# Converting w_out first, a second bank and an early split for its product with w3, two banks from the fourth token block on, and a planner that weighs the shared port

## The chip, the cores and the metric

The kernel runs on one core of one Trainium2 chip. The metric is device time in microseconds (us). In what follows PE is the matrix engine and PEld its weight load, DVE the vector engine, ACT the scalar engine, POOL GpSimd, SP the queue that issues the DMAs.

## The reference

Three layers follow one another: causal block attention (4 batches, 8 heads, 576 tokens, head size 64), then a gated product without activation, then a layer with an ELU.

```python
x = attention(q, k, v)            # block mask of 64, softmax; 2304 tokens x 512
a = x @ w1;  b = x @ w2           # 512 -> 1024
h = a * b @ w3                    # 1024 -> 1024
x = h @ w_out                     # 1024 -> 512
h = x @ w_in                      # 512 -> 2048
g = where(h > 0, h, exp(min(h, 0)) - 1)
out = g @ w_out2                  # 2048 -> 512
```

## The kernel before, in words

**Numbers in two parts.** Every matrix that PE multiplies in the second and third layer is held as a high part that PE reads exactly and a low part (the rest); a product is three matmuls (`PASSES`). Splitting activations costs a cast (ACT) and a subtraction (POOL). The weights come as 64-bit words; `convert` (L293) makes a unit of 128x512 of them: a DMA into a ring of four landing buffers, two ACT instructions (L322, L315), three DVE instructions (L328, L331, L336), one on POOL (L342 or L345), and for two-part results a cast on ACT (L373) and a subtraction on POOL or DVE (L351).

**Stage 1.** Sixteen attention units (`attention`, batch b and head pair hp), each with scores (L483, L538), maxima on DVE (L501, L546), exponentials on ACT (L508, L558), transposes on PE (L518, L569, L579), the product with v (L599), and reciprocals that go through a small transpose (L628) and DRAM before POOL scales the result (L650). Meanwhile 40 units of weights are converted: w_out (8), w3 (16), w1 and w2 together (16, `w12_units`). w_out and w3 are only multiplied with each other: `w_product` (L658) forms one of eight strips of w3 x w_out with 8 matmuls of 128x512 (two instructions each on PE) into the PSUM tile `wps` in bank 6, and splits it with an ACT cast (L677) and a DVE subtraction (L680). w3 strips lie in a ring of four (`RW`), and the slabs of w3 and w_out are taken over by the last weights of w1 and w2. So the second layer needs two products with weights per token, a, b (L767) and y (L731).

**Stage 2.** `block2(t)` handles 288 tokens, t = 0 to 7: split the input (`xs`, L707 on DVE, L712 on POOL; one buffer), eight times a, b and their product, and y in three parts (`PARTS`) of four outputs each; y is collected in `xy` by ACT (L745) or DVE (L751). Blocks 0 to 3 (`few`) use one PSUM bank each for a, b and y (5, 6, 7); from block 4 on each has two (5 and 0, 6 and 1, 7 and 3), of which 0, 1 and 3 belong to attention before. In the meantime the 32 units of the third layer's weights are converted; 12 of 16 slabs go to DRAM and come back when block 7 releases their place.

**Stage 3.** `block3(t)`, 384 tokens, six blocks: h (L839), ELU, split, and out (L874). Its inputs are split by L813 and L818 (`xa`, `xb`).

**What sets the order.** `Plan.run` (L125) lays all operations out once, at build time: each has an engine (some have a choice, `ways`), a cost, a priority (`prio`, smaller first) and dependences. Whenever an engine is free it gets the ready operation of smallest priority, and the engines then execute their lists in that order. Operations with `port=True` on DVE and POOL exclude each other in this calculation. Attention units 1 to 4 have priority -2500 and up, products -2400 and up, all conversions of stage 1 -1000 and up, later attention units 40 and up, PE's work of stage 2 10000 and up, and what empties PSUM in stage 2 about -10000. While PE would have nothing to do, and until the first product, the plan puts in filler matmuls (`spare`, L975).

```python
t = max(free[e], min(o.ready for o in ready[e]))
o = min((o for o in ready[e] if o.ready <= t), key=lambda o: (o.prio, o.n))
if o.ways[e][2]:
    t = max(t, port["POOL" if e == "DVE" else "DVE"])
```

Of the kernel before, what the change touches and what calls it, by code (L numbers as in the profile page):

```python
# [81 lines left out]
class Plan:  # L82
# [6 lines left out]
    def add(self, eng, us, fn, r=(), w=(), prio=0.0, port=False, after=(), lag=0.0, nbytes=0, ways=()):  # L89

        o = Op()
        o.eng, o.us, o.fn, o.prio, o.lag, o.nbytes = eng, us, fn, prio, lag, nbytes
        o.ways = {e: x for e, *x in ((eng, us, fn, port), *ways)}
        o.n = len(self.ops)
        deps = set(after)
        for key in r:
            if key in self.writer:
                deps.add(self.writer[key])
        for key in w:
            if key in self.writer:  # L100
                deps.add(self.writer[key])
            deps.update(self.readers.get(key, ()))
        for key in {*r, *w}:
            buf = key[0] if isinstance(key, tuple) else key
            if isinstance(buf, Buf):
                if key in w and buf.prev is not None:
                    deps.update(buf.prev.ops)
                elif buf.gate is not None:
                    deps.add(self.writer[buf.gate])
                buf.ops.append(o)  # L110
        for key in r:
            if key not in w:
                self.readers.setdefault(key, set()).add(o)
        for key in w:
            self.writer[key], self.readers[key] = o, set()
        deps.discard(o)
        o.deps, o.users = deps, []
        self.ops.append(o)
        return o
# [5 lines left out]
    def run(self):  # L125
        for o in self.ops:
            o.left, o.ready = len(o.deps), 0.0
            for d in o.deps:
                d.users.append(o)
        engines = ("GATE", "PE", "DVE", "ACT", "POOL", "SP")  # L130
        free = dict.fromkeys(engines, 0.0)
        ready = {e: [] for e in engines}
        for o in self.ops:
            if not o.left:
                for e in o.ways:
                    ready[e].append(o)
        pipe, port, done, lanes = 0.0, {"DVE": 0.0, "POOL": 0.0}, 0, [0.0] * self.LANES
        while done < len(self.ops):
            best = None
            for e in engines:  # L140
                if not ready[e]:
                    continue
                t = max(free[e], min(o.ready for o in ready[e]))
                o = min((o for o in ready[e] if o.ready <= t), key=lambda o: (o.prio, o.n))
                if o.ways[e][2]:
                    t = max(t, port["POOL" if e == "DVE" else "DVE"])
                if best is None or t < best[0]:
                    best = t, e, o
            t, e, o = best
            if e == "PE" and self.filler:  # L150
                self.filler(int((t - free[e] - 0.3) / 0.22))
            o.us, o.fn, shared = o.ways[e]
            o.eng = e
            for x in o.ways:
                ready[x].remove(o)
            if e == "SP":
                t = max(t, lanes.pop(0))
                pipe = max(pipe, t + 1.9) + o.nbytes / 390e3
                o.end, free[e] = pipe + 0.3, t + 0.45
                lanes.append(o.end)  # L160
            else:
                o.end = free[e] = t + o.us
                if shared:
                    port[e] = o.end
            o.fn()
            done += 1
            for u in o.users:
                u.ready = max(u.ready, o.end + (0.0 if [*u.ways] == [e] != ["SP"] else self.LAT[e] + u.lag))
                u.left -= 1
                if not u.left:  # L170
                    for x in u.ways:
                        ready[x].append(u)
        self.end = free
# [3 lines left out]
def attention_moe_moe2(  # L177
# [11 lines left out]
    nc = tc.nc  # L189
# [11 lines left out]
    add = plan.add  # L201
# [33 lines left out]
    def bank(k, base):  # L235
        banks[k] = Buf(lambda: psum, f"bank{k}", base, [P, 512], F32, banks[k])
        return banks[k]
# [3 lines left out]
    def turn(name, ks, base):  # L241
        n = turns.get(name, 0)
        turns[name] = n + 1
        return bank(ks[n % len(ks)], base)
# [15 lines left out]
    def wsl(s):  # L260
        return slab_buf[s]()
# [3 lines left out]
    W_S, WO_S, W3_S, RW = 0, 4, 6, 4  # L265
    w12_s = [8, 9, 10, 11, 6, 7, 4, 5]

    def full(s, i):
        return half_buf[s + i // 2]()[:, i % 2]

    def full_keys(s, i):
        return [(half_buf[s + i // 2], i % 2, h) for h in range(2)]
# [8 lines left out]
    def key3(m, x, h):  # L281
        return (hi_buf[m], x, h) if m < 4 else (slab_buf[order3[m - 4]], x, h)
# [373 lines left out]


    def w_product(i, prio):  # L658
        ps = turn("w", (6,), "wps")
        for j in range(KF):  # L660

            def mm(j=j):
                plan.filler = None
                a = full(W3_S, i % RW).rearrange("p (j c) -> p j c", c=P)
                bb = full(WO_S, j // 2).rearrange("p (j c) -> p j c", c=DM)[:, j % 2, :]
                nc.tensor.matmul(ps(), lhsT=a[:, j, :], rhs=bb, start=(j == 0), stop=(j == KF - 1))  # L666

            add(
                "PE", 0.86, mm,
                r=[*full_keys(W3_S, i % RW), *full_keys(WO_S, j // 2)], w=[ps], prio=prio,  # L670
            )

        def d():
            return wsl(W_S + i // 2).rearrange("p s (j c) -> p s j c", c=DM)[:, :, i % 2, :]

        k = [(slab_buf[W_S + i // 2], x, i % 2) for x in range(2)]
        add("ACT", 0.58, lambda: nc.scalar.copy(d()[:, 0, :], ps()), r=[ps], w=[k[0]], prio=prio)  # L677
        add(
            "DVE", 0.68,
            lambda: nc.vector.tensor_tensor(out=d()[:, 1, :], in0=ps(), in1=d()[:, 0, :].bitcast(F32), op=ALU.subtract),  # L680
            r=[ps, k[0]], w=[k[1]], prio=prio,
        )


# [12 lines left out]
    def block2(t):  # L697
# [6 lines left out]
        for k in range(KD):  # L704
# [3 lines left out]
                r=[(x, k, "n")], w=[(xs, k, 0)], prio=fast, port=True,  # L708
# [6 lines left out]
                r=[(x, k, "n"), (xs, k, 0)], w=[(xs, k, 1), (x, k, "s", h2)], prio=fast, port=True,  # L715
            )
        gs = []
        few = t < 4
        abanks, bbanks, ybanks = ((5,), (6,), (7,)) if few else ((5, 0), (6, 1), (7, 3))
        nm_ = "" if few else "+"  # L720

# [33 lines left out]
        for m in range(KF):  # L755
# [4 lines left out]
            def proj(ps, u, pr, m=m, wk=wk):  # L760
# [24 lines left out]
                r=[pb], w=[af], prio=fast,  # L785
# [128 lines left out]
    cp = -1000.0  # L914
    for n in range(NPAIR):
        attention(n, None)
    for h in range(2):
        for s in range(4):
            c = slice(h * 256, (h + 1) * 256)
            convert(  # L920
                wo_r[s][:, :, c], lambda x, s=s, c=c: full(WO_S, s).rearrange("p (j c) -> p j c", c=DM)[:, :, c],
                [[full_keys(WO_S, s)[h]]], cp, True,
            )

    def w12_units(ms, prio):
# [4 lines left out]
    for i in range(KF):  # L930
        for h in range(2):
            c = slice(h * HS, (h + 1) * HS)
            convert(
                w3T[i][:, c], lambda x, i=i, c=c: full(W3_S, i % RW)[:, c], [[full_keys(W3_S, i % RW)[h]]], cp + i, True
            )
        w_product(i, -2400.0 + i)
# [5 lines left out]
    for t in range(N2):  # L942
        block2(t)
    plan.gate("gate2", plan.ops[n1 - 1:])
    first3 = [block3_in(t) for t in range(2)]
    for m in range(KG):
        for h in range(2):
            if m < 4:
# [7 lines left out]
                r=[(st, 0), (st, 1)], w=[("wsc", m, h)], prio=2000.0 + m, nbytes=P * HS * 8,  # L956
            )
        if m >= 4:
            add(
                "SP", 0, lambda m=m: nc.sync.dma_start(out=slab3(m).bitcast(F32), in_=wsc[m - 4]),  # L960
                r=[("wsc", m, h) for h in range(2)], w=[key3(m, x, h) for x in range(2) for h in range(2)],
                prio=5000.0 + m, nbytes=P * 1024 * 8,
# [70 lines left out]
```

## Time and profile before

| | |
|---|---|
| median of 3 runs | 1012.65 us (1009.61 to 1014.29) |
| the profiled execution, its own time | 1009.9 us |
| its span, first to last instruction | 1008.1 us |
| mean granted clock of PE | 0.993 of 2.4 GHz |
| PE busy | 973.1 us (97% of the span) |
| DVE busy | 514.9 us (51%) |
| ACT busy | 425.2 us (42%) |
| POOL busy | 401.0 us (40%) |

A share over the whole span mixes stages of very different load; the rows below go by stretches. A busy PE is not the same as a useful one: the fillers count as busy, and matmuls are pipelined, so what a group of matmuls really takes is read from the distance between the starts of long groups.

### The profile page before, as it was taken

The page shows a single profiled execution, that of the slowest core. Times are in us where ns is not written, and L with a number is a line of the kernel's source. Part 1 is how long each engine was busy: PE and PEld are TensorE (multiplying, and loading weights), DVE is VectorE, ACT ScalarE, POOL GpSimd, SP SyncE. Part 2 cuts the span into 40 slices and gives each one's busy share as a digit, 9 for nine tenths or more (in the row PEclk, how much of TensorE's full clock was granted, in tenths as well). Part 3 has the DMA queues.
Part 4 walks back from the last instruction along what each step waited for, and adds up shares of the span by engine and source line. Part 5 has one row for each costly group of instructions (what it writes and reads, how often), then busy time and mean ns, then how long its engine had stood idle before and what let it go on. Part 6 is the DMA issues. An engine that isn't in the chain of part 4 may idle for free.

```text
span 1008.1 us, 16417 instructions
## 1 busy us (share of the span) xinstructions
PE 973.1 (97%) x6271; PEld 837.7 (83%) x6271; DVE 514.9 (51%) x998; ACT 425.2 (42%) x1017; POOL 401.0 (40%) x403
## 2 busy tenths in 40 slices
PE   9989799999999998999999999999999999999997
PEld 4544348888888898899999988888889988999996
DVE  6888798666565646677566142232332322422222
ACT  6676576655565534544544212222222222222222
POOL 4444565333233136767677232232232422322222
PEclk9999999999999999999999999999999999999999
DMA  6554652221221112355644860000000000000000
GB/s 222 172 162 160 195 169 88 72 73 48 72 71 49 37 55 84 126 172 175 210 157 166 300 243 1 1 32 1 1 32 1 22 11 1 32 1 1 33 1 31
DMA packets 39678, 87.64 MB, mean 87 GB/s; under 512 B 3744, under 2 KB 13360, under 8 KB 38064
## 3 DMA queue, kind: packets, MB, share of 16 engines
q1 hardware_dynamic: 39600, 86.60, 25.9%
q8 instruction: 49, 0.80, 0.3%
q14 instruction: 29, 0.24, 0.1%
HBM read 69.21 MB, written 17.38 MB: 86 GB/s over the span
## 4 chain that ended last, share of the span: by engine, by line
PE 83%; DVE 9%; DMA 4%; issue 1%; ACT 1%; POOL 1%; SPq 0%; POOLq 0%; ACTq 0%; DVEq 0%
PE o L874 20%; PE h L839 20%; PE b L767 10%; PE a L767 10%; PE y L731 9%; PE o L599 4%; PE s L483 3%; PE t L518 3%; DMA cr<-w 2%; DVE ct L336 1%; PE spare L975 1%; DMA scr<-rs 1%; DVE ct L328 1%; PE wps L666 1%; PE s L538 1%
## 5 line engine op out<-in xcount | busy, mean ns | idle before, releaser
L693 POOL TENSOR_TENSOR g<-e,g 128x384 fp32r<-128x384 f32 x96 | 97.6, 1017 | 277.8 <-ACT g L690 266.0
L851 DVE TENSOR_SCALAR e<-h 128x384 f32<-128x384 f32 x96 | 53.5, 557 | 225.3 <-PE h L839 224.8
L874 PE MATMUL o<-slab_lo,g 128*128 128x512 f32 x648 | 160.5, 396 | 0.8 <-POOL g L693 0.4
L855 ACT ACTIVATE e<-e 128x384 f32<-128x384 f32 x96 | 50.4, 525 | 241.8 <-DVE e L851 241.8
L874 PEld LDWEIGHTS o<-slab_lo,g 128*128 128x128 f32 x648 | 121.2, 188 | 26.7 <-POOL g L693 0.8
L731 PE MATMUL y<-g,slab_lo 128*128 128x288 f32 x768 | 120.4, 301 | 6.6 <-DVE xy L751 6.5
L767 PE MATMUL a<-xs,slab_lo 128*128 128x288 f32 x768 | 118.2, 298 | 0.0
L767 PE MATMUL b<-xs,slab_lo 128*128 128x288 f32 x768 | 117.3, 297 | 0.8 <-DVE af L784 0.8
L731 PEld LDWEIGHTS y<-g,slab_lo 128*128 128x128 f32 x768 | 107.4, 190 | 8.5 <-DVE xy L751 7.6
L767 PEld LDWEIGHTS b<-xs,slab_lo 128*128 128x128 f32 x768 | 106.7, 188 | 1.4 <-DVE af L784 1.0
L767 PEld LDWEIGHTS a<-xs,slab_lo 128*128 128x128 f32 x768 | 107.6, 189 | 0.3 <-issue 0.2
L693 POOL TENSOR_TENSOR g<-af,g 128x288 fp32r<-128x288 f32 x64 | 55.2, 863 | 114.4 <-ACT g L690 112.7
L342 POOL TENSOR_TENSOR ct<-ct,cr 128x512 int32<-128x512 int32 x48 | 67.1, 1398 | 35.5 <-DVE ct L336 17.8
L839 PE MATMUL h<-xa,slab_lo 128*128 128x384 f32 x432 | 80.6, 336 | 0.0
L839 PE MATMUL h<-xb,slab_lo 128*128 128x384 f32 x432 | 80.1, 339 | 0.0
L860 DVE SCALAR_TENSOR_TENSOR e<-e,h 128x384 f32<-128x384 f32 x96 | 53.2, 554 | 52.3 <-ACT e L855 52.2
L839 PEld LDWEIGHTS h<-xb,slab_lo 128*128 128x128 f32 x432 | 75.9, 188 | 2.9
L839 PEld LDWEIGHTS h<-xa,slab_lo 128*128 128x128 f32 x432 | 75.8, 188 | 2.9
L690 ACT CAST g<-e 128x384 fp32r<-128x384 f32 x96 | 49.3, 513 | 62.4 <-DVE e L860 61.8
L508 ACT ACTIVATE p<-s,st 128x128 f32<-128x128 f32 (+3 forms) x128 | 66.9, 528 | 14.9 <-DVE st L501 11.2
L501 DVE TENSOR_REDUCE st<-s 128x1 f32<-128x128 f32 (+3 forms) x128 | 57.4, 481 | 25.6 <-PE s L489 25.4
L666 PE MATMUL wps<-full,full 128*128 128x512 f32 x128 | 60.6, 617 | 9.3 <-DVE slab_lo L680 5.2
(90 smaller groups left out, 1479.8 us busy)
## 6 DMA issues: line engine op xcount, KB each, us to landing
cr<-w SPq DMA_DIRECT2D x48, 512.0 KB
wsc<-stage SPq DMA_DIRECT2D x24, 512.0 KB
slab_lo<-wsc SPq DMA_DIRECT2D x12, 1024.0 KB
cr<-w3T SPq DMA_DIRECT2D x16, 512.0 KB
raw<-qT SPq DMA_DIRECT2D x16, 288.0 KB
raw<-kT SPq DMA_DIRECT2D x16, 288.0 KB
rr<-scr SPq DMA_DIRECT2D x32, 144.0 KB
out<-ob SPq DMA_DIRECT2D x17, 256.0 KB
```

What stands on the lines that cost most here:

```text
L342: nc.gpsimd.tensor_tensor(out=t(), in0=t(), in1=words()[0], op=ALU.add)
L501: lambda s=s, c=c: nc.vector.tensor_reduce(out=nm(c), in_=s()[:, 0:nk], axis=AX.X, op=ALU.max, negate=True),
L508: lambda s=s, c=c, p=p: nc.scalar.activation(out=p()[:, 0:nk], in_=s()[:, 0:nk], func=AF.Exp, bias=nm(c), scale=1.0, accum_out=sm(c)),
L666: nc.tensor.matmul(ps(), lhsT=a[:, j, :], rhs=bb, start=(j == 0), stop=(j == KF - 1))
L693: lambda: nc.gpsimd.tensor_tensor(out=g()[:, 1, :], in0=src(), in1=g()[:, 0, :].bitcast(F32), op=ALU.subtract),
L731: nc.tensor.matmul(ps()[:, 0:T2], lhsT=w[:, a, n * P:(n + 1) * P], rhs=gs[m]()[:, c, :], start=(m == ms[0] and q == 0), stop=(m == ms[-1] ...
L767: nc.tensor.matmul(ps()[:, 0:T2], lhsT=w[:, a, u, k, :], rhs=xs()[:, k, c, :], start=(k == 0 and q == 0), stop=(k == KD - 1 and q == 2),)
L839: nc.tensor.matmul(ph()[:, 0:T3], lhsT=w[:, a, k, :], rhs=xs()[:, k, c, :], start=(k == 0 and q == 0), stop=(k == KD - 1 and q == 2),)
L851: "DVE", dve_us(T3), lambda e=e, ph=ph: nc.vector.tensor_scalar_min(e(), ph()[:, 0:T3], 0.0),
L855: "ACT", act_us(T3, True), lambda e=e: nc.scalar.activation(out=e(), in_=e(), func=AF.Exp),
L860: lambda e=e, ph=ph: nc.vector.scalar_tensor_tensor(out=e(), in0=e(), scalar=-1.0, in1=ph()[:, 0:T3], op0=ALU.add, op1=ALU.max),
L874: nc.tensor.matmul(acc(), lhsT=g()[:, a, s * P:(s + 1) * P], rhs=w[:, c, :], start=(m == 0 and q == 0), stop=(m == KG - 1 and q == 2),)
```

## The change

Five edits. The planner asks of each ready operation when it could start, the port included, and takes the smallest priority among those that can start first; an operation that waits for the port no longer holds back others. The product's tile takes banks 6 and 7 in turn. Its two splitting operations get priority -9000, ahead of all attention and conversion. `few` holds for blocks 0 to 2 only, so that block 3 has two banks each. The eight units of w_out get priority -3000, ahead of the first attention units.

```diff
-                t = max(free[e], min(o.ready for o in ready[e]))
-                o = min((o for o in ready[e] if o.ready <= t), key=lambda o: (o.prio, o.n))
-                if o.ways[e][2]:
-                    t = max(t, port["POOL" if e == "DVE" else "DVE"])
+
+                held = port["POOL" if e == "DVE" else "DVE"]
+                at = lambda o: max(free[e], o.ready, held if o.ways[e][2] else 0.0)
+                t = min(map(at, ready[e]))
+                o = min((o for o in ready[e] if at(o) <= t), key=lambda o: (o.prio, o.n))
...
-        ps = turn("w", (6,), "wps")
+        ps = turn("w", (6, 7), "wps")
...
-        add("ACT", 0.58, lambda: nc.scalar.copy(d()[:, 0, :], ps()), r=[ps], w=[k[0]], prio=prio)
+        add("ACT", 0.58, lambda: nc.scalar.copy(d()[:, 0, :], ps()), r=[ps], w=[k[0]], prio=-9e3)
...
-            r=[ps, k[0]], w=[k[1]], prio=prio,
+            r=[ps, k[0]], w=[k[1]], prio=-9e3,
...
-        few = t < 4
+        few = t < 3
...
-                [[full_keys(WO_S, s)[h]]], cp, True,
+                [[full_keys(WO_S, s)[h]]], -3000.0, True,
```

The whole list of every engine is laid out anew by this. Lines of the changed kernel are one higher from L145 on. Three places:

**PE, the first product** (`wps`: the tile of w3 x w_out; `t`, `s`, `o`: transposes, scores and v product of attention). Before, the first matmul of a product stands in the third attention unit, behind 95 fillers:

```order
L975 LDWEIGHTS mk
L975 MATMUL spare<-mk 128x512
L666 MATMUL wps_762<-full_203,full_698 128x512 x2
L518 MATMUL t_775<-ident,p_765 128x128 x3
L518 MATMUL t_781<-ident,p_772 128x128 x3
L483 MATMUL s_786<-k_329,q_311 128x512
```

In the changed kernel:

```order
L600 MATMUL o_417<-pt_325,v_112 64x256 x2
L600 MATMUL o_417<-pt_325,v_112 64x128 x2
L539 MATMUL s_427<-k_150,qb_85 128x288 x3
L667 MATMUL wps_437<-full_131,full_407 128x512 x2
L519 MATMUL t_448<-ident,p_440 128x128 x4
L519 MATMUL t_456<-ident,p_443 128x128 x4
L539 MATMUL s_462<-k_150,qb_85 128x288 x3
```

It now stands in the first attention unit, behind 102 fillers, 59 of which come before the first scores and 29 right behind these.

**PE, the end of the fourth attention unit** (its reciprocals' transpose reads `st`). Before, 19 of the 64 product matmuls are done by then, and most of the fifth unit lies among the others:

```order
L628 MATMUL t_1165<-ident,st_893 9x128
L666 MATMUL wps_1103<-full_203,full_884 128x512
L666 MATMUL wps_1103<-full_372,full_884 128x512 x4
L483 MATMUL s_1197<-k_931,q_842 128x256
L483 MATMUL s_1199<-k_931,q_842 128x256
```

In the changed kernel:

```order
L629 MATMUL t_1276<-ident,st_995 9x128
L667 MATMUL wps_1225<-full_131,full_407 128x512
L667 MATMUL wps_1225<-full_154,full_407 128x512 x4
L667 MATMUL wps_1307<-full_131,full_645 128x512 x4
L667 MATMUL wps_1307<-full_154,full_645 128x512 x4
L667 MATMUL wps_1347<-full_131,full_645 128x512 x4
L667 MATMUL wps_1347<-full_154,full_645 128x512 x4
L484 MATMUL s_1385<-k_982,q_904 128x256
```

43 of the 64 are done by then; the other 21 follow in one piece, the fifth unit and stage 2 behind them.

**DVE, from block 3 to block 4** (`xs`: block 4's input; `xy`<-`y`: emptying the bank of y; `ct`: a conversion). Before:

```order
L707 CAST xs_5219<-xy_2653 128x288
L751 TENSOR_TENSOR xy_1434<-y_5200,xy_1434 128x288
L707 CAST xs_5219<-xy_2653 128x288 x3
L331 TENSOR_SCALAR ct_5197<-ct_5197 128x512
L336 SCALAR_TENSOR_TENSOR ct_5197<-cr_5151,ct_5197 128x512
L751 TENSOR_TENSOR xy_1434<-y_5225,xy_1434 128x288
```

In the changed kernel:

```order
L708 CAST xs_5190<-xy_2781 128x288
L752 TENSOR_TENSOR xy_1654<-y_5173,xy_1654 128x288
L708 CAST xs_5190<-xy_2781 128x288 x2
L752 TENSOR_TENSOR xy_1654<-y_5186,xy_1654 128x288
L708 CAST xs_5190<-xy_2781 128x288
L752 TENSOR_TENSOR xy_1654<-y_5204,xy_1654 128x288
```

The instructions that empty y stand closer together, and their tiles lie in two banks.

## Rows read from the trace of the kernel before

**Rows 1.** Windows: PE, PEld, DVE, ACT, POOL busy (x instructions), clock, DMA share, GB/s
```profile
0.00:154.00 154.00, 136.42 (x737) 74.22 (x737) 125.12 (x238) 100.62 (x236) 77.41 (x80) 0.98 0.57 183
154.00:364.00 210.00, 209.05 (x1895) 180.50 (x1894) 131.19 (x309) 120.20 (x373) 67.45 (x75) 1.00 0.18 57
602.00:1008.00 406.00, 399.33 (x1975) 356.62 (x1974) 117.98 (x213) 103.20 (x199) 115.15 (x120) 1.00 0.03 12
```
**Rows 2.** Groups of PE's instructions, 0 to 160 us: busy, mean ns | idle before, releasers
```profile
L666 PE MATMUL wps<-full,full 128*128 128x512 f32 x128 | 60.6, 617 | 9.3 <-DVE slab_lo L680 5.2 <-POOL ct L342 3.0 <-POOL full L345 0.9
L483 PE MATMUL s<-k,q 64*128 64x256 f32 (+2 forms) x132 | 17.5, 354 | 2.6 <-ACT p L558 1.8 <-ACT p L508 0.7
L599 PE MATMUL o<-pt,v 128*64 128x256 f32 (+3 forms) x220 | 17.3, 296 | 1.5 <-ACT pt L407 1.2 <-DVE pt L408 0.2
L518 PE MATMUL t<-ident,p 128*128 128x128 f32 x100 | 17.0, 283 | 2.2 <-ACT p L508 2.1
```
**Rows 3.** Timeline of PE and its weight loads, the first stage: start, us
```profile
1.98 8.04 PE L975 MATMUL spare<-mk 128*128 128x512 bf16 x25 [1.98 <-POOL mk L903]
...
7.05 2.47 PEld L975 LDWEIGHTS <-mk 128*128 128x128 bf16 x12 [0.25 <-issue]
...
54.80 1.52 PE L666 MATMUL wps<-full,full 128*128 128x512 f32 x3
...
89.28 2.04 PE L666 MATMUL wps<-full,full 128*128 128x512 f32 x2 [2.03 <-DVE slab_lo L680]
...
113.44 8.49 PE L666 MATMUL wps<-full,full 128*128 128x512 f32 x16 [2.99 <-POOL ct L342]
...
145.75 7.11 PE L666 MATMUL wps<-full,full 128*128 128x512 f32 x16 [1.60 <-DVE slab_lo L680]
```
**Rows 4.** Groups of PE's instructions, 154 to 364 us
```profile
L599 PE MATMUL o<-pt,v 128*64 128x256 f32 (+3 forms) x520 | 39.1, 294 | 0.2 <-ACT pt L407 0.2
...
L767 PE MATMUL a<-xs,slab_lo 128*128 128x288 f32 x240 | 38.2, 301 | 0.0
...
L731 PE MATMUL y<-g,slab_lo 128*128 128x288 f32 x192 | 34.3, 309 | 0.0
```
**Rows 5.** The chain that ended last, one piece of stage 2: start, us
```profile
363.44 1.60 PE a L767 x12
```
**Rows 6.** Groups of DVE's instructions, 0 to 154 us
```profile
L331 DVE TENSOR_SCALAR cp<-ct 128x512 int32<-128x512 int32 x32 | 22.1, 691 | 0.8
L336 DVE SCALAR_TENSOR_TENSOR ct<-cr,cp 128x512 int32<-128x512 int32 x32 | 21.8, 681 | 0.7
L328 DVE TENSOR_SCALAR ct<-ct 128x512 f32<-128x512 f32 x36 | 21.4, 594 | 6.6 <-ACT ct L322 6.6
L501 DVE TENSOR_REDUCE st<-s 128x1 f32<-128x128 f32 (+3 forms) x40 | 17.8, 479 | 2.7 <-PE s L489 2.6
L408 DVE COPY pt<-t 128x128 f32<-128x128 f32 (+4 forms) x23 | 9.6, 432 | 3.8 <-PE t L518 2.9 <-PE t L579 1.0
...
L707 DVE CAST xs<-xy 128x288 fp32r<-128x288 f32 x4 | 5.8, 1438 | 3.9 <-POOL xy L650 3.9
```
**Rows 7.** Timeline of PE from block 2 to 3 and from block 3 to 4
```profile
387.46 1.46 PE L731 MATMUL y<-g,slab_lo 128*128 128x288 f32 x9 [2.14 <-DVE xy L751]
...
425.47 1.46 PE L731 MATMUL y<-g,slab_lo 128*128 128x288 f32 x9 [0.55 <-DVE xy L751]
430.03 2.35 PE L731 MATMUL y<-g,slab_lo 128*128 128x288 f32 x9 [3.10 <-DVE xy L751]
432.18 1.64 PE L767 MATMUL a<-xs,slab_lo 128*128 128x288 f32 x6
```
**Rows 8.** The tile xa, its casts: ns min/median/max, first and last start
```profile
L813 DVE CAST xa<-xy x16: 245/350/1186, 367.1 to 797.7; 128x384 fp32r<-128x384 f32 x8, 128x192 fp32r<-128x192 f32 x8
```
**Rows 9.** Timeline of DVE, a conversion's L328 at its shortest
```profile
97.32 0.42 DVE L328 TENSOR_SCALAR ct<-ct 128x512 f32<-128x512 f32 x1
```

## The prediction

> **What bounds the kernel now.** I read the busy time by windows first. From 154 to 364 us PE is busy for 209.05 of 210 us, and in stage 3 for 399.33 of 406 us; before 154 us only for 136.42, much of that with fillers [rows 1]. So from about 154 us on PE is the bound and has little to give; the time can change through what PE has done of use by then, and at the few later places where it stops. Second, PE's waits by groups show what it stops for in the front: product matmuls wait 9.3 us, 5.2 of these for the split L680 to empty the only bank and 3.9 for a conversion on POOL; attention's matmuls wait 2.6, 1.5 and 2.2 us, nearly all for ACT [rows 2]. Third, PE's timeline shows the last product ending at 145.75 + 7.11 = 152.9 us [rows 3], and the only larger stops of stage 2, where one block hands over to the next [rows 7].
>
> **The front, as a ledger of PE.** Prices: 16 product matmuls in 7.11 us are 0.444 us each, so 128 take 56.9 us; fillers take 8.04 us for the first 25 (half clock at first), then 2.47/12 = 0.206 each [rows 3]; a, b and y matmuls take 1.60/12 = 0.133 each [rows 5]. An attention unit: between 154 and 364 us there are 240 + 240 + 192 of a, b (as many as a), y (89.6 us), which leaves 119.5 of 209.05 us to some 11 units (of 16 in all, the first four and most of the fifth lie before; the 520 v products, at 44 a unit, give 11.8), thus 10.9 us [rows 1, 4].
>
> Before, up to 152.9 us: start 1.98, 95 fillers 22.4, four units 43.6, products 56.9, most of the fifth unit (all but 36 of its v products and a few transposes) 7.8, six matmuls of a 0.8: 133.5 us. The other 19.4 us are lost: 9.3 + 6.3 of waits [rows 2], some 2.8 at half clock (16 product matmuls behind the wait of 2.99 us took 8.49 us and not 7.11, and another stretch begins behind the wait of 2.03) [rows 3], and 1.0 unnamed.
>
> After, by the new order, the 64 products end with four units done and none of the fifth. That is 8.6 us less work, so the change breaks even here if the products end at 152.9 - 8.6 = 144.3 us. Bounds: with no loss at all 1.98 + 23.9 (102 fillers) + 43.6 + 56.9 = 126.4 us, a gain of 17.9. If all waits stay except those for the split, which the second bank and the early priority remove, and except the half clock that followed them: 126.4 + 11.4 = 137.8, a gain of 6.5. What would hold PE to such a time is DVE, 81% busy before 154 us [rows 1]. Up to the last split its list is shorter by 3 conversions (1.97 us each), 8 maxima (0.479) and 12 copies (0.432), 14.9 us together, which now stand behind it [rows 6]. With the idle share unchanged that makes 154 x (125.1 - 14.9)/125.1 = 135.7 us, and 134 for the last product, which ends some 1.5 us sooner. I take this one, since DVE's row is the nearest to a bound: **10 us gained**, with 0 (DVE and ACT lose as much elsewhere) and 17.9 as the ends.
>
> What is moved ahead pays too. SP issues four w_out transfers, 2 MB, before q and k. The first scores stand behind 59 fillers, which end at 1.98 + 8.04 + 34 x 0.206 = 17 us; q and k have until then, and the fillers are counted in the 102.
>
> **The planner's rule.** A DVE instruction that shares the port lasts longer when POOL is running: L328 takes 0.594 us on average against 0.42 where nothing stands against it [rows 6, 9], in 36 instructions 6.3 us, and four L707 take 1.438 each [rows 6]. The new rule puts other work there in the plan. I give it nothing. The Trainium skill (SBUF — State Buffer, Who interferes with whom) says that the pair is an exclusive lock, that whoever starts first holds it for the whole instruction, and that issue order decides who blocks; by that, a list laid out from computed start times gets the time back only where the chip keeps to them. Were all 6.3 us regained, DVE would allow 128 instead of 135.7, and PE's floor of 126.4 would be reached: the upper end of the range above.
>
> **Block 3 to block 4.** Before, y has one bank, and the DVE list puts three casts of xs and a conversion ahead of the instruction that empties it: waits of 0.55 and 3.10 us, then half clock, where 9 matmuls of y took 2.35 us against 1.46, and 6 of a 1.64 us against 1.06 (six distances and the same 0.26 of tail) [rows 7]. With two banks both go: 0.55 + 3.10 + 0.89 + 0.58 = **5.1 us gained**. The lower end is 0, if DVE is late by a whole block; the upper end is 5.1. The two banks are free in time: PE's list ends attention before block 3's first matmul.
>
> **Block 2 to block 3** keeps one bank, and keeps its wait of 2.14 us [rows 7] in some form. New is that four casts of xa stand among the instructions that empty y, 0.35 us each in the middle and 1.186 at most [rows 8]; two groups of six matmuls (1.6 us) cover part. I put **1 us lost**, between 3.1 lost (four times 1.186, less the cover) and 2.1 gained (the wait, covered by the last attention unit).
>
> All later boundaries have two banks before and after, and stage 3 is the same work: nothing.
>
> **Sum:** -10 - 5.1 + 1 = -14.1 us on the profiled execution's 1009.9, thus 995.8. That execution lies 2.75 below the median of the runs; on their scale the forecast is 1012.65 - 14.1 = 998.5, say **998 us**.
>
> **Rivals.**
> *The front only changes its shape.* DVE, ACT and POOL carry the same 40 conversions, and the w_out units come at the expense of attention, so that the products end at 144 us after all. For it: DVE at 81% and ACT at 65% would have to rise [rows 1]. Against it: the split's 5.2 us of waits has no other cause than the bank. Time: 1012.65 - 4.1 = 1008.5. Chance 0.17.
>
> *Slower: PE stalls at the first product.* It now stands in the first attention unit, and PE executes in order, so the rest of attention stands behind ten conversions (8 of w_out, 2 of w3). Without a wait PE reaches it at about 31 us (17, then 43 more fillers, 8.9, and about half an attention unit, 5.5). DVE alone needs 20 us for ten conversions. If it starts at 54.80 as before [rows 3], everything shifts by some 23 us, the products end at 157, and the loss is 12.7 - 4.1 = 8.6: 1021 us. It breaks even with a first product at 45 us and is slower by half a per cent from 50. Against it: the eight of w_out now go ahead of all attention, where before they came behind the first four units. Chance 0.11.
>
> *The front gains, the boundaries don't*: block 2 to 3 takes over what block 3 to 4 loses. Time 1012.65 - 10 = 1003. Chance 0.10.
>
> **How the numbers follow.** The forecast has 0.62, with its own range 987 to 1006. Half a per cent, 5 us, is about what a measurement of this kernel can tell from no change; that bound is 1007.6. Faster: 0.60 of the forecast, the third rival's 0.10 and a quarter of the first's, 0.74. Slower: the second rival, 0.11 less a little, 0.11 with what I have not thought of. Same: the rest, 0.15. The range runs from 987 (all of the front's floor, less what a plan always loses on the chip) to 1010 (the first rival and the scatter of the runs); it leaves out the slower rival and some 0.04 below.
>
> **What would show it.** Right: the last `wps` matmul ends near 134 us (126 to 140), no wait of PE for L681 (L680 before), the first product between 28 and 36 us, no stop of 3 us between blocks 3 and 4, PE full in between. Wrong: a first product after 45 us, PE waiting for POOL's conversions in the front for over 15 us, or new stops of several us in stage 2, which was full before and has nothing to give but much to lose from a list laid out anew.

## The result and the profile after

| | before | changed |
|---|---|---|
| median | 1012.65 us (1009.61 to 1014.29) | **983.14 us** (982.01 to 983.71, 4 runs) |
| ratio | | 0.9711, 95% interval 0.9686 to 0.9735 |
| profiled execution, its span | 1009.9, 1008.1 us | 983.31, 981.5 us |

Faster, by twice the forecast and below its range. The span is shorter by 26.6 us. To see where, both traces are cut at two places of PE's order that they have in common: the end of the products (`wps`) and the last group of y. The busy times by windows (us; window, its length, then PE, PEld, DVE, ACT and POOL busy with their instructions, the granted clock, DMA share, GB/s), first of before, newly cut:

```profile
0.00:152.90 152.90, 135.32 (x725) 73.42 (x726) 124.40 (x236) 99.52 (x234) 77.41 (x80) 0.98 0.57 182
152.90:594.06 441.16, 432.75 (x3545) 402.28 (x3544) 266.68 (x537) 220.97 (x582) 204.69 (x199) 1.00 0.36 120
594.06:1008.10 414.04, 405.03 (x2005) 362.00 (x2004) 123.86 (x226) 104.68 (x202) 118.92 (x124) 0.99 0.04 16
```

and of the changed kernel, where [rows 1] had the stretches of before:

```profile
0.00:125.00 125.00, 121.98 (x664) 65.35 (x664) 109.40 (x199) 88.63 (x205) 66.99 (x71) 1.00 0.61 199
125.00:572.29 447.29, 441.64 (x3614) 409.64 (x3613) 288.83 (x576) 232.40 (x616) 207.62 (x203) 0.99 0.36 125
572.29:981.50 409.21, 403.13 (x2005) 360.77 (x2004) 122.33 (x226) 104.75 (x202) 117.74 (x124) 1.00 0.05 17
```

The front is 27.9 us shorter, of which the forecast's ledger takes off 8.6 for attention work that now lies behind it (an estimate; that work was not measured by itself): **-19.3**. The middle is 6.1 longer, less the same 8.6: **-2.5**. Stage 3 gives **-4.8**. Idle time of PE (length less busy) fell from 17.6 to 3.0 us in the front, 8.4 to 5.7 in the middle, and 9.0 to 6.1 in stage 3.

What PE waited for up to the products' end (total, times, longest), the six largest of nine in before:

```profile
PE wps L666 <- DVE slab_lo L680: 5.2, 3, 2.0
PE wps L666 <- POOL ct L342: 3.0, 1, 3.0
PE t L518 <- ACT p L508: 2.1, 2, 1.8
PE spare L975 <- POOL mk L903: 2.0, 1, 2.0
PE s L483 <- ACT p L558: 1.8, 1, 1.8
PE o L599 <- ACT pt L407: 1.2, 2, 0.6
```

and, all there is, in the changed kernel:

```profile
PE spare L976 <- POOL mk L904: 2.0, 1, 2.0
PE t L519 <- ACT p L509: 1.0, 2, 0.7
```

All waits of products are gone, whether for the split or for POOL, and nearly all of attention's. PE's timeline of the changed kernel (start, duration, group), at the places of [rows 3]:

```profile
1.98 14.22 PE L976 MATMUL spare<-mk 128*128 128x512 bf16 x59 [1.98 <-POOL mk L904]
...
31.95 1.88 PE L667 MATMUL wps<-full,full 128*128 128x512 f32 x4
...
106.86 18.19 PE L667 MATMUL wps<-full,full 128*128 128x512 f32 x42
124.98 0.62 PE L484 MATMUL s<-k,q 64*128 64x256 f32 x6
```

The first product starts at 31.95 us, the last ends at 125.0. Behind it comes something new, on PE:

```profile
131.06 0.48 PE L519 MATMUL t<-ident,p 128*128 128x128 f32 x1 [2.02 <-ACT p L509]
...
132.48 1.81 PE L768 MATMUL a<-xs,slab_lo 128*128 128x288 f32 x6
```

on DVE at that time:

```profile
124.55 1.86 DVE L451 SCALAR_TENSOR_TENSOR k<-raw,k 128x576 fp32r<-128x576 f32 x1
...
128.31 1.40 DVE L332 TENSOR_SCALAR ct<-ct 128x512 int32<-128x512 int32 x1
129.64 0.68 DVE L681 TENSOR_TENSOR slab_lo<-wps,slab_lo 128x512 fp32r<-128x512 f32 x1
130.24 0.47 DVE L502 TENSOR_REDUCE st<-s 128x1 f32<-128x128 f32 x2
```

and on POOL:

```profile
124.11 1.69 POOL L343 TENSOR_TENSOR ct<-ct,cr 128x512 int32<-128x512 int32 x1 [0.40 <-DVE ct L337]
128.07 1.35 POOL L343 TENSOR_TENSOR ct<-ct,cr 128x512 int32<-128x512 int32 x1 [2.28 <-issue]
```

The fifth unit's maxima (L502) stand behind two DVE instructions that last as long as POOL's beside them: L332 takes 0.43 us alone at 126.78, and 1.40 here. PE then waits 2.02 us, and six matmuls of a take 1.81 us, where at full clock they take 0.96 (at 412.10, below). From 129 to 139 us the granted clock averages 0.66, which by an estimate costs 10 x 0.34 = 3.4 us; it is 0.98 during the wait and 0.50, the lower of its two levels, from 131.06 to 137.70.

Block 3 to block 4, the place of the second part of [rows 7], and then the entrance of stage 3:

```profile
406.14 6.12 PE L732 MATMUL y<-g,slab_lo 128*128 128x288 f32 x42
412.10 0.96 PE L768 MATMUL a<-xs,slab_lo 128*128 128x288 f32 x6
...
572.29 0.96 PE L732 MATMUL y<-g,slab_lo 128*128 128x288 f32 x6
573.09 3.29 PE L840 MATMUL h<-xa,slab_hi 128*128 128x384 f32 x18
576.21 2.27 PE L875 MATMUL o<-slab_hi,g 128*128 128x512 f32 x9
578.32 2.25 PE L840 MATMUL h<-xa,slab_hi 128*128 128x384 f32 x12
```

and that entrance in before, which no row ahead of the prediction shows:

```profile
594.06 0.96 PE L731 MATMUL y<-g,slab_lo 128*128 128x288 f32 x6
594.86 3.28 PE L839 MATMUL h<-xa,slab_hi 128*128 128x384 f32 x18
600.38 1.85 PE L839 MATMUL h<-xa,slab_hi 128*128 128x384 f32 x6 [2.24 <-DVE e L860]
602.03 4.26 PE L874 MATMUL o<-slab_hi,g 128*128 128x512 f32 x13
```

Before, 24 matmuls of h follow one another, the last six 2.24 us late and then at a granted clock of 0.67; o comes only after them. Now nine matmuls of o stand in between, and nothing is waited for. Of the 4.8 us of stage 3, 2.9 are idle time of PE, and 1.9 are busy time, the matmuls behind the old stop having run at the lower clock.

### The profile page after: what moved, and what is told of

Read it like the earlier page. It is cut to its first block, busy times and chain, and to the rows that moved or that the text cites. A ratio compares the mean times of both kernels' runs of the same rounds, so it can differ in the third digit from the quotient of the medians.

```text
span 981.5 us, 16441 instructions
## 1 busy us (share of the span) xinstructions
PE 966.7 (98%) x6278; PEld 835.8 (85%) x6278; DVE 520.6 (53%) x1000; ACT 425.8 (43%) x1022; POOL 392.3 (40%) x396
## 4 chain that ended last, share of the span: by engine, by line
PE 83%; DVE 7%; DMA 4%; POOL 3%; issue 2%; ACT 1%; SPq 0%; POOLq 0%; DVEq 0%; ACTq 0%
PE h L840 20%; PE o L875 20%; PE a L768 8%; PE b L768 8%; PE y L732 8%; PE o L600 4%; PE s L484 4%; PE t L519 3%; PE wps L667 2%; DMA cr<-w3T 1%; PE s L539 1%; DVE ct L337 1%; DVE ct L329 1%; POOL ct L343 1%; DMA cr<-wo 1%
## 5 line engine op out<-in xcount | busy, mean ns | idle before, releaser
L732 PE MATMUL y<-g,slab_lo 128*128 128x288 f32 x768 | 116.8, 300 | 2.1 <-DVE xy L752 2.0
L694 POOL TENSOR_TENSOR g<-af,g 128x288 fp32r<-128x288 f32 x64 | 57.2, 894 | 114.0 <-ACT g L691 112.7
L502 DVE TENSOR_REDUCE st<-s 128x1 f32<-128x128 f32 (+3 forms) x128 | 56.5, 482 | 22.3 <-PE s L490 22.1
```

The costliest lines, as they stand in the source:

```text
L502: lambda s=s, c=c: nc.vector.tensor_reduce(out=nm(c), in_=s()[:, 0:nk], axis=AX.X, op=ALU.max, negate=True),
L694: lambda: nc.gpsimd.tensor_tensor(out=g()[:, 1, :], in0=src(), in1=g()[:, 0, :].bitcast(F32), op=ALU.subtract),
L732: nc.tensor.matmul(ps()[:, 0:T2], lhsT=w[:, a, n * P:(n + 1) * P], rhs=gs[m]()[:, c, :], start=(m == ms[0] and q == 0), stop=(m == ms[-1] ...
```

## The experiments

Each kernel was timed in three rounds beside the kernel before (1010.2, 1011.5 and 1010.3 us median for the first four, the next four and the last four). The differences below are of medians, across rounds whose base differs by up to 2.4 us; by the ratios, what undoing an edit costs comes out 1.4 to 3.2 us larger. The columns in the middle are of the profiled executions and cut as above: where the products end, PE's idle time up to there, then the lengths of the middle and of stage 3.

| kernel | median us | ratio, 95% interval | products end | PE idle | middle | stage 3 |
|---|---|---|---|---|---|---|
| before | 1012.65 | | 152.9 | 17.6 | 441.2 | 414.0 |
| changed | 983.14 | 0.9711, 0.9686 to 0.9735 | 125.0 | 3.0 | 447.3 | 409.2 |
| without w_out first | 990.44 | 0.9815, 0.9792 to 0.9839 | 131.8 | 7.0 | 446.8 | 409.2 |
| with one bank | 1004.87 | 0.9940, 0.9916 to 0.9964 | 147.0 | 15.0 | 449.0 | 409.1 |
| without the rule | 988.63 | 0.9791, 0.9769 to 0.9813 | 126.5 | 2.3 | 447.3 | 414.1 |
| block 3 in the old form | 988.92 | 0.9799, 0.9774 to 0.9824 | 126.1 | 3.5 | 454.8 | 409.1 |
| without the early split | 985.50 | 0.9752, 0.9736 to 0.9767 | 124.8 | 3.4 | 449.1 | 409.7 |
| before + banks, early split | 1001.96 | 0.9910, 0.9891 to 0.9929 | 130.8 | 7.1 | 455.6 | 412.7 |
| before + w_out first | 1019.89 | 1.0092, 1.0075 to 1.0109 | 146.1 | 13.7 | 456.9 | 414.2 |
| before + the rule | 1002.76 | 0.9912, 0.9894 to 0.9930 | 151.0 | 12.9 | 437.4 | 409.6 |
| before + all three of the front | 996.50 | 0.9853, 0.9813 to 0.9893 | 126.4 | 2.2 | 455.5 | 412.6 |
| before + block 3's form | 1008.06 | 0.9965, 0.9938 to 0.9991 | 152.6 | 16.7 | 441.3 | 414.1 |
| changed, w_out second | 987.48 | 0.9754, 0.9715 to 0.9794 | 130.5 | 4.7 | 445.8 | 409.2 |
| changed, plan cost alone | 986.22 | 0.9743, 0.9704 to 0.9781 | 130.8 | 7.1 | 444.1 | 409.2 |

How much of the fifth unit lies ahead of the products' end differs, so first and middle column are to be read together.

**Four parts undone, one each.** Three theories of the front: that converting w_out first fills PE's gaps with products (A), that the second bank does it (B), or that the planner's rule lets DVE keep up (C).

```diff
-                [[full_keys(WO_S, s)[h]]], -3000.0, True,
+                [[full_keys(WO_S, s)[h]]], cp, True,
```

> The changed kernel with w_out's units back behind the first four attention units; the other four edits stay. Theory A (w_out first is what fills the gaps of PE in all four attention units with product matmuls, and so gives the front): the first product starts at 45 to 58 us, the products end at 140 to 150 instead of 125, total 998 to 1006 us. Theory B (the second bank and the early split give the front): the products end by 130 and the total stays at 982 to 989.

```diff
-        ps = turn("w", (6, 7), "wps")
+        ps = turn("w", (6,), "wps")
```

> The changed kernel with the product's tile in bank 6 alone; the early split and the rest stay. Theory A: PE waits 3 to 6 us for the split's DVE instruction between products, and the time is 985 to 991 us. Theory B: the products pile up at the end as before, 995 us or more.

The third takes back the planner's lines of the change's diff, and nothing else.

> The changed kernel with the planner's old choice. Theory A: DVE is not what ends the front, so the front stays at 125 to 130 us and the total at 982 to 989 us. Theory C (DVE kept up with PE only because instructions that wait for the shared port no longer hold back others): the products end at 133 or later, total 991 us or more.

```diff
-        few = t < 3
+        few = t < 4
```

> The changed kernel with one bank each for block 3's a, b and y again. By the prediction's term: waits of 0.5 and 3 us return where block 3 hands over to block 4, with a stretch at half clock, 986.5 to 989.5 us. Rival: the new list has moved the casts away from the instructions that empty y, the stop is under 1 us, and the time stays within 1 us of 983.1.

Undoing w_out's place costs 7.3 us, undoing the bank 21.7. With one bank the waits for the split are back; PE's waits by groups up to the products' end:

```profile
PE wps L667 <- DVE slab_lo L681: 6.1, 3, 4.7
PE o L600 <- DVE pt L409: 3.2, 2, 1.9
```

and the longest in its timeline:

```profile
106.50 7.03 PE L667 MATMUL wps<-full,full 128*128 128x512 f32 x16
...
118.84 5.73 PE L667 MATMUL wps<-full,full 128*128 128x512 f32 x8 [4.70 <-DVE slab_lo L681]
```

Eight product matmuls behind the stop take 5.73 us, 16 before it 7.03: the granted clock of these 5.73 us is 0.64, and 1.00 before the stop. So the bank is the condition of the front's gain. Without the rule the front is that of the changed kernel (126.5 us, 2.3 us idle): C falls there. A's marks (products' end at 140 to 150, 998 to 1006 us) were missed by far and B's (130, 989) by little, so B holds, with A as the smaller part. The 5.5 us that the rule's absence costs lie mostly in stage 3 (4.9 us longer), whose entrance reads as in the kernel before:

```profile
574.63 3.28 PE L839 MATMUL h<-xa,slab_hi 128*128 128x384 f32 x18
580.15 2.29 PE L839 MATMUL h<-xa,slab_hi 128*128 128x384 f32 x6 [2.24 <-DVE e L860]
```

Block 3 in its old form costs 5.8 us in the median, and PE's timeline shows the stop where [rows 7] had it:

```profile
409.95 1.46 PE L732 MATMUL y<-g,slab_lo 128*128 128x288 f32 x9 [0.55 <-DVE xy L752]
413.72 1.46 PE L732 MATMUL y<-g,slab_lo 128*128 128x288 f32 x9 [2.30 <-DVE xy L752]
417.17 2.53 PE L732 MATMUL y<-g,slab_lo 128*128 128x288 f32 x9 [1.99 <-DVE xy L752]
```

**Parts put alone into the kernel before, and the early split undone.** The edits are those of the change's diff: the two banks with the early split; w_out's priority; the changed kernel with its split at `prio`; the planner's lines.

> The kernel before with two banks for the product and its early split, nothing else. Theory B2 (with one bank PE has no product matmul to fill gaps with from the end of a product until DVE has split it, eight times over, and the plan then lets the products pile up behind attention): most of the front's gain comes back, the products end at 128 to 136 us with none of the fifth attention unit ahead of them, total 994 to 1002. Theory A2 (banks and w_out first are worth little apart, each needs the other): 1004 or more.

> The kernel before with w_out first, nothing else. Theory B2: the bank still holds the products back, so they end at 145 to 153, 1003 to 1013 us. Theory A2: the same as B2 here, since the bank is missing. Theory A (the earlier one): 990 to 997.

> The changed kernel with the split at the product's own priority, two banks. Theory B2 with the bank alone: one bank is being emptied while the other fills, so a late split costs little, 982 to 988 us. Rival (the early split does it, the bank only follows): DVE splits late behind maxima and conversions, PE waits for it over 5 us, 991 or more.

> The kernel before with the planner's new choice alone. Theory C2 (the rule is worth some 5 us at the entrance of stage 3, where casts of xb no longer stand ahead of the ELU's instruction): PE's wait of 2.2 us there is gone, stage 3 is 4 to 5 us shorter, 1005 to 1009 us in all. Rival (that wait comes and goes with any new list): the wait is there or not, and the time is 1008 to 1015 with gains and losses elsewhere.

The banks and the early split bring the products' end from 152.9 to 130.8 us; the middle takes 14.4 of these 22.1 us back, a good part of it work of the fifth unit that has moved there (8.6 in the ledger), and waits for y among the rest (8.1 us, 6.5 in before). **w_out first, alone, is slower** by 0.9%, which none of the theories had: its products wait for the one bank longer than before, and behind the front y waits (6.5 us in before). PE's waits by groups up to the products' end, and behind the line of dots from there to the last y:

```profile
PE wps L666 <- DVE slab_lo L680: 8.0, 4, 3.1
...
PE y L731 <- DVE xy L751: 11.0, 9, 2.9
```

The clock adds to it: from the products' end to the last y, the time that PE does not get for its granted clock (length times one less the clock, added up over windows of 5 us) is 8.5 us, against 1.7 in before. So one and the same edit costs 8.4 us with one bank, and gains 5.5 with two (996.50 against 1001.96; 7.3 in the changed kernel). The rule alone gains 8.7 us in the median; of the 10.1 us of its profiled span 4.4 lie in stage 3, where o stands between the h groups as in the changed kernel, and the rest ahead of it, in no one place; the median lies below the 1005 us expected at best. The early split is worth 2.4 us by the medians, which the last experiment shows to be within what a new order does by itself.

**Do the parts add, and what is chance?** The first of these four is the kernel before with the three edits of the front, without the rule and with block 3 as it was; the second has only `few = t < 3`. The other two start from the changed kernel:

```diff
-                [[full_keys(WO_S, s)[h]]], -3000.0, True,
+                [[full_keys(WO_S, s)[h]]], -2499.0, True,
```

```diff
-            add("POOL", 1.28, c5, r=[rk2, t], w=keys[0], prio=prio, port=True)
+            add("POOL", 1.35, c5, r=[rk2, t], w=keys[0], prio=prio, port=True)
...
-        add("POOL", 1.28, c5, r=[rk2], w=[t], prio=prio, port=True)
+        add("POOL", 1.35, c5, r=[rk2], w=[t], prio=prio, port=True)
```

> The kernel before with the three edits of the front (w_out's casts first, the two banks, the early split), and neither the planner's rule nor the short form of block 3. Theory 1 (the edits' effects lie at separate places and add: front about -19 by w_out and the banks, rule about -5 at stage 3's entrance, short block 3 about -5 at its boundary): products end 124 to 128 us, stage 3 from the last group's first y to the end 412 to 415 us, a stop or a half-clock stretch at blocks 3 and 4 as before; median 993 to 997. Theory 2 (the rule keeps DVE level in the front too, and without it the first edits lose a part): products end 130 us or later, median 998 or more. Theory 3 (what differs between these lists is chance of the planner's order, not the edits): no such sum, the median anywhere from 985 to 1005 with waits at other places.

> The kernel before with block 3 in the short form alone. Theory 1 (block 3's short form frees the banks that block 4's first groups want, so the stop of 3 us and the half-clock stretch after it go): front unchanged (products end 151 to 154), the span's gain about 5 us between blocks 3 and 4, median 1005 to 1009. Theory 2 (the short form only helps where the front has already been shortened, as in the changed kernel): within 2 us of the kernel before, or slower, as block 3's own groups then wait for their single banks.

> The changed kernel with w_out's casts and loads put just behind the first q and k loads of the units, instead of ahead of all of them: the first scores stand behind 25 spare matmuls in place of 59, the first product behind 109. Theory 1 (what w_out first gives is products to run while DVE and ACT hold the first units up; it is enough that it comes soon): products end within 2 us of the changed kernel's 125.0, median 981 to 986. Theory 2 (w_out ahead of q and k only costs the start, and the spares there are time lost): products end 119 to 123, median 977 to 981, better than both kernels. Theory 3 (the products come too late to fill the early gaps): products end 128 to 132 as without w_out first (131.75), median 987 to 991.

> The changed kernel with nothing changed but one cost that the planner holds for a GpSimd step (1.28 to 1.35 us): every instruction is the same, some stand in another order. It measures what a mere new order is worth. Theory 1 (the differences of 5 us and more in the other runs come from their edits): median within 2 us of the changed kernel's 983.1, products end 124 to 127, stage 3 409 to 410. Theory 2 (such differences are chance of the order): median 3 us or more away, with new waits at places that no edit touches.

The three edits of the front, without the rule, bring the whole of the front (126.4 us, 2.2 idle), as the first theory had it; the median of 996.5 is 13.4 above the changed kernel's, of which 5.5 + 5.8 were found by undoing rule and block form one at a time. w_out behind the first q and k ends the products at 130.5 and is 4.3 us slower, within the third theory's numbers; that speaks against the second, by which the start is time lost. A mere new order, with the same instructions, moved the median by 3.1 us, past the 2 of the first theory, and the products' end by 5.8, to 130.8, with new waits of 0.96 and 1.19 us for DVE at the end of the third unit and 1.68 at the end of the fourth. So **differences of some 3 us between these kernels, and of some 6 us in the products' end, carry no mechanism** by themselves. The run with w_out second can't be told from this one, and the 6.8 us that undoing w_out's place adds to the products' end hardly; that w_out first gains with two banks rests on two medians (5.5 and 7.3). What is held to the bank (22.0 us of products' end), to block 3's form and to the rule has, besides, its place in a trace: the products' waits, the stop at block 4, the entrance of stage 3.

Block 3's form alone gained only 0.35% (2.3 us; expected 5), no more than a new order, and its profiled span is that of before (1008.0 us). Its stop shrank from 3.10 to 0.97 us, but the clock fell at the boundary before. PE's timeline there with block 3's form alone:

```profile
387.32 2.53 PE L731 MATMUL y<-g,slab_lo 128*128 128x288 f32 x9 [2.15 <-DVE xy L751]
389.65 1.64 PE L767 MATMUL a<-xs,slab_lo 128*128 128x288 f32 x6
```

its busy times in the window 386 to 394:

```profile
386.00:394.00 8.00, 6.68 (x29) 6.68 (x30) 4.19 (x6) 1.93 (x3) 4.09 (x4) 0.57 0.03 5
```

and six matmuls of a and the same window in before, with a wait of 2.14 at the same instruction [rows 7]:

```profile
388.76 0.96 PE L767 MATMUL a<-xs,slab_lo 128*128 128x288 f32 x6
...
386.00:394.00 8.00, 6.54 (x49) 6.54 (x50) 5.51 (x9) 2.90 (x6) 4.71 (x5) 1.00 0.09 26
```

No kernel of the twelve beats the changed one.

## Why the prediction was right, and where it was wrong

**The front: its waits right, its term mis-sized.** The forecast gave 10 us, with 17.9 as the most; it was 19.3. The step that failed is the one that let DVE hold PE back "with the idle share unchanged". What DVE had to do up to the last split was counted well: 125.1 us of busy time less 14.9 makes 110.2, and 109.40 were measured by 125.0 us. But its idle share fell from 18.6% of 152.9 us to 12.5% of 125.0, and PE came to its own floor: of the 19.3 us, 14.6 are idle time of PE and 3.4 granted clock (added up as above: 3.4 us in before, none now). The floor was put at 126.4 and found at 125.0, with 1.0 us of waits in it: a product matmul was priced at 0.444 us with the tail of its group, and in the long group above they follow each other at 0.43, 2 us less over 128. (For the first fillers, "half clock" is the forecast's word: they stand under a granted clock of 1.00 up to 8 us.) The waits for POOL and ACT, which the ledger's other way kept (137.8 us), went as well.

Which edit did this, the parts put alone into the kernel before tell. Their windows up to the products' end, first with the banks and the early split, then with w_out first:

```profile
0.00:130.80 130.80, 123.71 (x657) 66.19 (x657) 104.80 (x200) 85.27 (x198) 68.51 (x74) 0.99 0.60 189
0.00:146.10 146.10, 132.36 (x707) 70.45 (x707) 125.70 (x224) 95.33 (x220) 74.63 (x78) 0.98 0.59 188
```

With the banks PE's idle time falls from 17.6 to 7.1 us, and no product waits any more, for the split or for POOL; that holds in all nine kernels with two banks. DVE's idle share is 19.9% there: it did not fall, and PE, with 5.1 us of idle time behind the start, came near its floor all the same (DVE was busy for 104.8 us by then). With w_out first alone DVE's idle share is 14.0%, and PE is idle for 13.7 us. With both and without the rule it is 12.4%, and PE is idle for 2.2. Over all the kernels DVE's share is 12.0 to 16.8% where w_out comes early, and 17.1 to 20.3% where it does not. So the bank took the products' waits away, and DVE's gaps closed with w_out's place and not with the bank; how w_out's place closes them no run shows. The old idle share of DVE was no bound on PE.

The Trainium skill (PSUM — Partial Sum Buffer, PSUM bank collisions raise a hardware error) says that two engines must not access the same part of a bank at a time, and that the guard is a semaphore by bank. With one bank the trace shows PE waiting in this way for L681 (here the product that lies in the bank also has to be read before the next is written), and the run gives the price: single waits of up to 4.70 us, and a granted clock of 0.64 behind the longest.

**The first product** was put at about 31 us and came at 31.95. With that the slower rival, which needed 45 us, fell. It was not empty: w_out first, with one bank, does lose, though at another place, in waits for the bank and for y and in clock, not before the first product.

**The planner's rule: "I give it nothing"** was right for the front and wrong for the kernel. Groups of DVE from 0 to 126 us (count, then busy us, mean ns, idle before it), in the changed kernel

```profile
L329 DVE TENSOR_SCALAR ct<-ct 128x512 f32<-128x512 f32 x32 | 20.6, 643 | 2.3 <-ACT ct L323 2.2
L451 DVE SCALAR_TENSOR_TENSOR k<-raw,k 128x576 fp32r<-128x576 f32 x6 | 7.3, 1217 | 0.0
L708 DVE CAST xs<-xy 128x288 fp32r<-128x288 f32 x4 | 3.3, 829 | 2.3 <-POOL xy L651 2.3
```

and without the rule

```profile
L328 DVE TENSOR_SCALAR ct<-ct 128x512 f32<-128x512 f32 x33 | 21.1, 640 | 0.2 <-ACT ct L322 0.2
L450 DVE SCALAR_TENSOR_TENSOR k<-raw,k 128x576 fp32r<-128x576 f32 x5 | 6.6, 1324 | 0.0
L707 DVE CAST xs<-xy 128x288 fp32r<-128x288 f32 x4 | 3.4, 845 | 3.0 <-POOL xy L650 3.0
```

last alike (L708 is shorter than in [rows 6] with the rule and without it; the rule alone in the kernel before leaves L329 at 605 ns against 594): the plan does not win back the time that DVE spends behind POOL. The rule of the Trainium skill that the forecast cited (SBUF — State Buffer, Who interferes with whom) agrees with the second row of POOL above: L332 starts 0.24 us after that instruction, ends 0.29 us after it, and so lasts 1.40 us in place of 0.43. What the forecast missed is that the rule lays out the whole list anew, far from the port: all eight kernels with it have 409.1 to 409.7 us of stage 3 and an o group ahead of the h that waits, all six without it 412.6 to 414.2.

**Block 3 to block 4:** 5.1 us foreseen, the stop gone, and 5.8 us when undone. Right in the changed kernel; alone in the kernel before, 2.3.

**Block 2 to block 3:** 1 us lost was foreseen; the wait of 2.14 us went instead and the one of 0.55 stayed. In the changed kernel the casts of xs stand ahead of the instructions that empty y there and the casts of xa behind them. Small, and of the wrong sign; which edit did it was not tried.

**"Stage 3 is the same work: nothing"** failed: the same work, but not the same order, 4.8 us. And stage 2, called full, lost 2.0 + 3.4 us at 129 to 139, which the gains at the two boundaries more than made up: over the whole middle PE's idle time fell by 2.7 us, while the clock cost 1.7 more (added up as above, 3.4 against 1.7). That makes -1.0 of the -2.5 measured for the middle; the other 1.5 us are not assigned.

In all, -14.1 was foreseen, and -26.6 measured on the profiled execution: 9.3 of the difference lies in the front, where PE's floor and not DVE's idle share set the time, and 4.8 at the entrance of stage 3; the middle gave 1.6 less than foreseen.

## What to carry to other kernels

When a wait sits in a loop of engines (a bank that one fills and another empties), price its removal by the floor of the engine that stops. The old idle share of another engine is not a bound: here it stayed as it was with the bank alone, and the engine that stops came near its floor all the same. Where a planner lays out the lists, look in the new order at every place where PE stopped before, also where the edit has no business, and put a null edit beside the experiments to know what a new order is worth by itself (here some 3 us of the median, and 6 of a place inside). Edits can be conditions of one another: try them alone and undone before calling one good.

## What was not expected of the hardware

Equal waits did not give equal clocks. In the kernel before and in the one with block 3's form alone, PE waits 0.55 and 2.1 us for the same instructions at 383 to 387 us; behind them the one has a granted clock of 1.00 in the window shown, the other 0.57, with six matmuls of a in 0.96 and in 1.64 us. By an estimate from these windows (8 us times 0.43) a stop can thus cost some 3.4 us more or nothing at all; what decides it the runs do not tell.
